# Experts' token tables from one-hot products on TensorE in place of scattered writes, key and query products on two engines, gate logits in column strips

## The chip, the cores and the metric

The kernel runs on one core of one Trainium2 chip. The metric is the device time of one execution in microseconds (us), less is better. The core's engines each run a queue of their own: TensorE (PE; its weight loads are PEld), VectorE (DVE), ScalarE (ACT), GpSimd (POOL) and SyncE (SP), which issues most DMAs. The profile gives one execution; "q" behind an engine (SPq) is its issuing side.

## The reference

Three layers follow each other on 3072 tokens (4 sequences of 768) with 384 features (8 heads of 48):

```python
# attention: a state of 48x48 for each of 32 heads, decayed by alpha
state = alpha[:, :, t, :, None] * state + einsum('bhd,bhe->bhde', k[:, :, t], v[:, :, t])
y[:, :, t] = einsum('bhd,bhde->bhe', q[:, :, t], state)
# mixture of 8 experts: 384 -> 1024 -> 384, two experts for each token
noisy = x @ w_gate + log1p(exp(x @ w_noise)) * noise
top2, weights = two largest of noisy, softmax of the two
for e in range(8):
    out[mask] += weights * (relu(x[mask] @ w1[e]) @ w2[e])
# last layer: 384 -> 2048 -> 384 with a leaky relu
out = max(0.01 * (x @ w_in), x @ w_in) @ w_out
```

## The kernel before

**Order.** A planner (class `Planner`) writes out the order of all engines' queues before anything runs. Each step has an engine (or two to choose from, "vg" for DVE or GpSimd), an expected duration, steps that it waits for, buffers that it takes from rings of a fixed count, and a due time, which is passed back from successors. The planner takes the engine that can start earliest and on it the ready step with the earliest due time. So a changed duration or wait also moves other steps. Queues then run in that order, each instruction waiting for its semaphores. Steps of phase 1 (attention, routing, first gathers) are placed until the last tile has been turned; then phase 2 (experts, last layer) follows, with what is left of phase 1 in between.

**Attention** (phase 1). 24 units of 128 tokens, eight heads each in 112 partitions. For each unit DVE scans the decay backwards (`suf`) and forwards (`wt`, two scans, the second operand in PSUM), and multiplies keys (`kt`, line 918) and queries (`qp`, line 922) by them. TensorE turns the keys (930), makes the scores (943: 48 rows in either half of the array, eight products of 128 columns), updates the state (975, 979) and makes the output `pY` (996 within the unit, 1001 across units). ScalarE copies PSUM to SBUF; GpSimd masks the scores (`am`, 952), decays the state (`sp`, 968) and makes two small products of totals.

**Routing** (phase 1 for six tiles of four units). TensorE turns a tile of x in 12 transposes (1040), ScalarE copies it to `xt` (one buffer), TensorE makes the logits of 16 columns (1050: three products with 512 moving columns), ScalarE copies them, four small transposes bring tokens back to the partitions (1059). A chain of some 30 small steps, most on DVE, picks two experts for each token and, with a triangular product on TensorE (1119, 1120), counts each choice's place in its expert's queue. `si` (1141) is the row of the table that belongs to the choice. GpSimd then writes token numbers with eight indirect DMAs for each tile (1148), 128 numbers each, into the table `idx_d` in DRAM, 48 in all.

**Experts** (phase 2). Each expert has two groups of slots, 384 and 480 rows. SyncE loads the table back (`load_idx`, 505): an early one, of the first four tiles, for the first groups of experts 0 and 1; two later ones for the rest. GpSimd gathers the tokens' rows of x by it (510), TensorE turns them (528), then come the hidden products (668) and the output products (707), in fp32r with every operand split into a high and a low part (three matmuls for one). Rows go to `y_d`; the last layer gathers two rows for each token (730), adds them with the gate's weights and does the same kind of products.

A slot's row in the table is interleaved by blocks: 480 slots are four blocks of 120.

## Time and profile before

| | us |
|---|---|
| median of the 3 timed runs | 1103.73 |
| their lowest and highest | 1098.47, 1114.14 |
| the profiled execution, whole | 1096.46 |
| its span, first to last instruction | 1094.7 |

The span is what the views of the trace show; 1.8 us of the profiled execution lie around it. TensorE's busy time is modelled (pipelined matmuls), so it is read together with its idle time in a stage and with the granted clock, a share of full speed: 1.00 is 2.4 GHz, 0.50 is 1.2 GHz.

### The profile page before, as it was taken

What the parts mean: (1) busy time and instruction counts of PE and PEld (TensorE: products, weight loads), DVE (VectorE), ACT (ScalarE), POOL (GpSimd) and SP (SyncE); (2) the same over time, 40 slices, a digit from 0 to 9 for tenths busy, and PEclk for the clock granted to TensorE, in tenths of its full rate; (3) what the DMA queues carried; (4) which work ended last, traced back from release to release, by engine and by line L of the source; (5) the groups of instructions that cost most, each with busy time, mean ns of one, the idle gap of its engine ahead of it and who ended that gap; (6) DMA issues with size and microseconds to landing.
All of it is one profiled execution on the core that took longest, in us unless ns stands there. A gap on an engine that the chain in (4) does not pass through costs nothing.

```text
span 1094.7 us, 17345 instructions
## 1 busy us (share of the span) xinstructions
PE 1068.6 (98%) x6404; PEld 1017.5 (93%) x6404; DVE 586.8 (54%) x1199; ACT 389.1 (36%) x829; POOL 324.6 (30%) x386
## 2 busy tenths in 40 slices
PE   7999998999999999999999999999999999999997
PEld 6877886899999999999999999999999999999997
DVE  8588974522445554754565334554555555454543
ACT  3665553322344453533453333231222212121211
POOL 3457766531113333444253131320111102010000
PEclk9999896999999999999999999999999999999999
DMA  9868832233345364655566555320101111100000
GB/s 245 239 180 194 176 82 86 39 92 107 121 124 184 125 208 148 209 168 154 172 206 226 198 190 181 115 66 7 59 12 55 29 37 30 37 23 22 1 23 25
DMA packets 76965, 125.76 MB, mean 115 GB/s; under 512 B 10407, under 2 KB 57383, under 8 KB 76871
## 3 DMA queue, kind: packets, MB, share of 16 engines
q1 hardware_dynamic: 68679, 104.47, 31.9%
q0 software_dynamic: 8192, 20.09, 6.5%
q8 instruction: 52, 0.85, 0.3%
q14 instruction: 42, 0.34, 0.1%
HBM read 91.84 MB, written 32.69 MB: 114 GB/s over the span
## 4 chain that ended last, share of the span: by engine, by line
PE 93%; POOL 2%; issue 2%; DVE 1%; ACT 1%; DMA 1%; POOLq 0%; ACTq 0%; DVEq 0%
PE py L707 40%; PE ph L668 39%; PE pY L996 3%; PE pA L528 2%; PE pS L943 2%; PE pY L1001 2%; PE pM L975 1%; PE pA L1050 1%; PE pM L979 1%; DMA at<-in_al_l_dram 1%; PE pM L930 1%; PE pA L1040 1%; POOL am L952 1%; POOL idx_d L1148 1%; DVE kt L918 0%
## 5 line engine op out<-in xcount | busy, mean ns | idle before, releaser
L692 DVE SCALAR_TENSOR_TENSOR hl<-ph,hh 128x384 fp32r<-128x384 f32 (+1 forms) x128 | 77.6, 606 | 202.7 <-ACT hh L685 186.6
L678 ACT ACTIVATE hc<-ph 128x384 f32<-128x384 f32 x128 | 62.9, 492 | 294.9 <-PE ph L668 289.6
L681 DVE SCALAR_TENSOR_TENSOR hc<-hc 128x384 f32<-128x384 f32 x128 | 71.5, 558 | 174.6 <-ACT hc L678 173.0
L685 ACT ACTIVATE hh<-ph 128x384 fp32r<-128x384 f32 (+1 forms) x128 | 68.0, 531 | 261.3 <-PE ph L668 247.8
L707 PE MATMUL py<-w2hA,hh 128*128 128x384 f32 (+1 forms) x416 | 142.1, 342 | 0.0
L707 PE MATMUL py<-w2hB,hh 128*128 128x384 f32 (+1 forms) x416 | 141.7, 341 | 0.0
L707 PE MATMUL py<-w2hA,hl 128*128 128x384 f32 (+1 forms) x416 | 140.5, 338 | 0.0
L707 PE MATMUL py<-w2lA,hh 128*128 128x384 f32 (+1 forms) x416 | 140.2, 337 | 0.0
L707 PE MATMUL py<-w2lB,hh 128*128 128x384 f32 (+1 forms) x416 | 140.0, 337 | 0.0
L707 PE MATMUL py<-w2hB,hl 128*128 128x384 f32 (+1 forms) x416 | 140.0, 337 | 0.0
L668 PE MATMUL ph<-xh,w1hA 128*128 128x384 f32 (+1 forms) x384 | 136.0, 354 | 0.9 <-issue 0.9
L668 PE MATMUL ph<-xl,w1hA 128*128 128x384 f32 (+1 forms) x384 | 134.2, 350 | 0.2 <-issue 0.2
L668 PE MATMUL ph<-xh,w1hB 128*128 128x384 f32 (+1 forms) x384 | 133.9, 349 | 0.0
L668 PE MATMUL ph<-xh,w1lA 128*128 128x384 f32 (+1 forms) x384 | 133.9, 349 | 0.0
L668 PE MATMUL ph<-xl,w1hB 128*128 128x384 f32 (+1 forms) x384 | 133.6, 348 | 0.0
L668 PE MATMUL ph<-xh,w1lB 128*128 128x384 f32 (+1 forms) x384 | 133.5, 348 | 0.0
L730 POOL DMA_INDIRECT xg<-y_d,gidx x48 | 48.7, 1015 | 263.2 <-PE pA L528 212.5
L510 POOL DMA_INDIRECT xg<-x_d,idx x56 | 55.7, 994 | 106.4 <-PE pA L528 87.0
L707 PEld LDWEIGHTS py<-w2hA,hh 128*128 128x128 f32 (+1 forms) x416 | 77.3, 186 | 1.2 <-issue 0.3
L707 PEld LDWEIGHTS py<-w2lA,hh 128*128 128x128 f32 (+1 forms) x416 | 77.3, 186 | 0.9
L707 PEld LDWEIGHTS py<-w2lB,hh 128*128 128x128 f32 (+1 forms) x416 | 77.3, 186 | 1.0
L707 PEld LDWEIGHTS py<-w2hB,hh 128*128 128x128 f32 (+1 forms) x416 | 77.3, 186 | 0.8
(153 smaller groups left out, 1989.0 us busy)
## 6 DMA issues: line engine op xcount, KB each, us to landing
w1s<-in_moe_w_dram SPq DMA_DIRECT2D x32, 384.0 KB
w2s<-in_moe_w_dram SPq DMA_DIRECT2D x32, 384.0 KB
kq<-in_kq_l_dram SPq DMA_DIRECT2D x24, 448.0 KB
w1s<-in_moe_w_in_dram SPq DMA_DIRECT2D x24, 256.0 KB
w2s<-in_moe_w_out_dram SPq DMA_DIRECT2D x16, 384.0 KB
y_d<-ys SPq DMA_DIRECT2D x32, 180.0 KB
at<-in_al_l_dram SPq DMA_DIRECT2D x24, 226.2 KB
nv<-in_v_l_dram SPq DMA_DIRECT2D x24, 192.0 KB
```

The lines of the kernel that those rows point to most:

```text
L510: nc.gpsimd.indirect_dma_start(out=xg[:n, :], out_offset=None, in_=x_d[0:rows, :], in_offset=bass.IndirectOffsetOnAxis(ap=idx_sb[i][:n, j, ...
L528: nc.tensor.transpose(p[:, d, :n], src[:n, d * 128:(d + 1) * 128], identf[:n, :n])
L668: nc.tensor.matmul(ps[:, :n], a[:, d, fo:fo + 128], x[:, d, :n], start=i == 0, stop=i == len(seq) - 1)
L678: nc.scalar.activation(hc[:, :n], ps[:, :n], AF.Copy)
L681: nc.vector.scalar_tensor_tensor(hc[:, :n], hc[:, :n], 0.01, hc[:, :n], op0=OP.mult, op1=OP.max)
L685: nc.scalar.activation(hh[:, :n], ps[:, :n], AF.Relu)
L692: nc.vector.scalar_tensor_tensor(hl[:, :n], ps[:, :n], 0.0, hh[:, :n].bitcast(FT), op0=OP.max, op1=OP.subtract)
L707: nc.tensor.matmul(py[:n, :], h[:, o:o + n], w[:, f % 2, :], start=(f == 0 and i == 0), stop=(f == nf - 1 and i == 2))
L730: nc.gpsimd.indirect_dma_start(out=yg, out_offset=None, in_=y_d[0:rows, :], in_offset=bass.IndirectOffsetOnAxis(ap=gidx[:, c, kk:kk + 1], ...
L943: nc.tensor.matmul(d["pa", i][:, p], d["kt"][r, p], d["qp"][r, p], start=True, stop=True)
L996: nc.tensor.matmul(d["py"][:, p, i * D:(i + 1) * D], d["am"][:, i, p, :], d["v"][:, h * D:(h + 1) * D], start=h == 0, stop=first, skip_gro ...
L1001: nc.tensor.matmul(d["py"][:, p, :], d["qp"][:, p], d["sp"][:, p].rearrange("p s d -> p (s d)"), start=False, stop=True, skip_group_check= ...
```

## The change

- `idx_d`, its zeroing, the scatters and the three index loads are gone. For each tile three integer operations on DVE split the slot number into a row (0 to 127) and a column (block and expert, 56 in all). DVE compares a row of counts with them: one-hot rows (128 wide) and one-hot columns (56 wide) in bf16, for four token columns and two choices. The one-hot columns are multiplied by the token's position in its column of 128 and by the number of that column (DVE or GpSimd). Eight bf16 matmuls sum row x column products over the tile's tokens (`table`), 112 columns; DVE adds the sum to `places`, and one DVE step, `indices`, makes token numbers of it. That step stands where an index load stood: one early, after four tiles, one late.
- The one-hot rows and columns use the one `xt` buffer, and a tile's turning takes that buffer before its first transpose.
- Key and query products may run on DVE or GpSimd, as the planner finds.
- The logits of a tile are made in four strips of 32 columns of the array, one for each unit, 12 products of 128 columns; the gate's weights are padded to 32 columns. One copy of 128x128 and one transpose bring them back.
- 480 slots are three blocks of 128 and one of 96, not interleaved.
- Expected durations for the state's update, logits and copies are changed.

```diff
-    idx_d = dram.tile([1 + E * CAP, 1], I32, name="idx_d")
...
+    NBLK = -(-CAP // 128)
+    tok = consts.tile([128, NCH, 2], FT)
+    count = consts.tile([128, 128], I32)
+    places = consts.tile([128, 2, NBLK * E], FT)
+    idx_sb = [consts.tile([128, NBLK, E], U32, name=f"idx{i}") for i in range(2)]
...
-    GB = [blocks_of(g) for g in GR]
+    GB = [[(o, min(128, g - o)) for o in range(0, g, 128)] for g in GR]
...
-    def load_idx(i, g):
-        src = slots_of(idx_d, g).rearrange("p j e o -> p (j e o)")
-        nc.sync.dma_start(idx_sb[i][:GB[g][0][1]].rearrange("p j e -> p (j e)"), src.bitcast(U32))
+    def indices(i):
+        nc.vector.scalar_tensor_tensor(idx_sb[i].rearrange("p j e -> p (j e)"), places[:, 1], 128.0, places[:, 0],
+                                       op0=OP.mult, op1=OP.add)
...
-        late_in = [add("s", 0.07, lambda g=g: load_idx(g, g), list(scat), lat=2.3) for g in (1, 0)]
+        late_in = add("v", 0.25, lambda: indices(1), list(placed))
...
-            kk = add("v", 0.86, keys, [b1], use=[(LK, R["kq"]), (b0, R["suf"])], takes=[R["kt"]])
-            qq = add("v", 0.9, queries, [f1], use=[(LK, R["kq"]), (f0, R["wt"])], takes=[R["qp"]])
+            kk = add("vg", dict(v=0.86, g=1.35), keys, [b1], use=[(LK, R["kq"]), (b0, R["suf"])], takes=[R["kt"]])
+            qq = add("vg", dict(v=0.9, g=1.35), queries, [f1], use=[(LK, R["kq"]), (f0, R["wt"])], takes=[R["qp"]])
...
-                up = add("p", 0.72, update, use=[(ck, R["kN"]), (LV, R["nv"])], takes=[R["pM"]], due=b + 3.2)
+                up = add("p", 0.9, update, use=[(ck, R["kN"]), (LV, R["nv"])], takes=[R["pM"]], due=b + 3.2)
...
             def logits():
-                k["pl"] = ps2.tile([2 * E, TT], FT, name="pA")
+                k["pl"] = ps2.tile([128, C], FT, name="pA")
                 for d in range(KD):
-                    nc.tensor.matmul(k["pl"], wgn[:, d, :], k["xt"][:, d, :], start=(d == 0), stop=(d == KD - 1))
+                    for c in range(NG):
+                        nc.tensor.matmul(k["pl"][32 * c:32 * c + 32, :], wgn[:, d, :], k["xt"][:, d, c * C:(c + 1) * C],
+                                         start=(d == 0), stop=(d == KD - 1), skip_group_check=True)
...
-                for c in range(NG):
-                    nc.tensor.transpose(k["pb"][:, c, :], k["lt"][:, c * C:(c + 1) * C], identf[:2 * E, :2 * E])
+                nc.tensor.transpose(k["pb"].rearrange("p c e -> p (c e)"), k["lt"], identf)
...
-                tx = add("p", 0.46, lambda d=d: turn_x(d), xs[T] + before, use=[(xs[T][0], R["x"])], takes=[R["pA"]],
-                         due=b + 2 + 2 * d)
+                tx = add("p", 0.46, lambda d=d: turn_x(d), xs[T] + ([t0] if d else before), use=[(xs[T][0], R["x"])],
+                         takes=[R["pA"]] + ([] if d else [R["xt"]]), due=b + 2 + 2 * d)
...
-            lg = add("p", 1.35, logits, [consts_in] + cp, use=[(cp[0], R["xt"])], takes=[R["pA"]], due=b + 8)
-            cl = add("a", 0.6, copy_l, [lg], use=[(lg, R["pA"]), (cp[0], R["xt"])])
-            tb = add("p", 0.35, turn_back, [cl], use=[(cp[0], R["xt"])], takes=[R["pA"]], due=b + 10)
+            lg = add("p", 0.8, logits, [consts_in] + cp, use=[(t0, R["xt"])], takes=[R["pA"]], due=b + 8)
+            cl = add("a", 0.28, copy_l, [lg], use=[(lg, R["pA"]), (t0, R["xt"])])
+            tb = add("p", 0.2, turn_back, [cl], use=[(t0, R["xt"])], takes=[R["pA"]], due=b + 10)
...
-            def scatter(kk, c):
-                ins = nc.gpsimd.indirect_dma_start(
-                    out=idx_d[:, :], out_offset=bass.IndirectOffsetOnAxis(ap=keep["si"][:, kk, c:c + 1], axis=0),
-                    in_=tok[:, c0 + c:c0 + c + 1], in_offset=None, bounds_check=E * CAP, oob_is_err=False)
...
+            def split_slot():
+
+                keep["row"], keep["col"] = (rt.tile([128, 2, n], U32, name=nm) for nm in ("row", "col"))
+                nc.vector.tensor_scalar(keep["row"], keep["si"], 3, 127, op0=OP.logical_shift_right, op1=OP.bitwise_and)
+                nc.vector.tensor_scalar(keep["col"], keep["si"], 10, 3, op0=OP.logical_shift_right,
+                                        op1=OP.logical_shift_left)
+                nc.vector.scalar_tensor_tensor(keep["col"], keep["si"], 7, keep["col"], op0=OP.bitwise_and,
+                                               op1=OP.bitwise_or)
+
+            def one_hot(what):
+                if what == "row":
+                    buf = early.tile([128, KD, TT], FT, name="xt", bufs=1).rearrange("p d c -> p (d c)").bitcast(BF)
...
+                src = keep[what].bitcast(I32)
+                for k in range(2):
+                    nc.vector.tensor_tensor(out[:, k], count[:, None, 0:m].to_broadcast([128, n, m]),
+                                      src[:, k, :, None].to_broadcast([128, n, m]), op=OP.is_equal)
+
+            def numbers(en):
+                eng = nc.vector if en == "v" else nc.gpsimd
+                for k in range(2):
+                    for w in range(2):
+                        eng.tensor_mul(keep["vals"][:, k, :, w, :], keep["cols"][:, k],
+                                       tok[:, c0:c0 + n, w:w + 1].to_broadcast([128, n, NBLK * E]))
+
+            def table():
+                keep["pt"] = ps2.tile([128, 2 * NBLK * E], FT, name="pA")
+                for i in range(2 * n):
+                    k, c = divmod(i, n)
+                    nc.tensor.matmul(keep["pt"], keep["rows"][:, k, c], keep["vals"][:, k, c].rearrange("p w f -> p (w f)"),
+                                     start=i == 0, stop=i == 2 * n - 1)
+
+            def collect():
+                pl = places.rearrange("p w f -> p (w f)")
+                nc.vector.tensor_add(pl, keep["pt"], pl)
...
-            sc = [add("g", 1.29, lambda kk=kk, c=c: scatter(kk, c), [sl] + late, lat=2.2,
-                      due=1e9 if late else at_unit(4 * gr[-1] + 5) + RDUE + 25 + 1.3 * (2 * c + kk)) for c in range(n) for kk in range(2)]
-            scat.extend(sc)
+            kw = {} if late else dict(due=at_unit(4 * gr[-1] + 5) + RDUE + 25)
+            ss = add("v", 0.6, split_slot, [sl], **kw)
+            h0 = add("v", 1.15, lambda: one_hot("row"), [ss], takes=[R["xt"]], **kw)
+            h1 = add("v", 0.6, lambda: one_hot("col"), [ss], use=[(h0, R["xt"])], **kw)
+            nb = add("vg", dict(v=1.2, g=2.0), numbers, [h1], use=[(h0, R["xt"])], **kw)
+            tb = add("p", 0.6, table, [nb], use=[(h0, R["xt"])], takes=[R["pA"]], **kw)
+            co = add("v", 0.25, collect, placed[-1:] + late, use=[(tb, R["pA"])], **kw)
+            placed.append(co)
...
-                early_in = add("s", 0.07, lambda: load_idx(2, 0), list(scat), lat=2.3)
+                early_in = add("v", 0.25, lambda: indices(0), list(placed))
```

## Rows read from the trace of the kernel before

**Rows 1.** The page: busy time of each engine, share of span, instructions.

```profile
PE 1068.6 (98%) x6404; PEld 1017.5 (93%) x6404; DVE 586.8 (54%) x1199; ACT 389.1 (36%) x829; POOL 324.6 (30%) x386
```

**Rows 2.** Stages: length, busy (instructions) of five engines, TensorE clock, DMA, GB/s.

```profile
24.68:163.72 139.04, 133.88 (x1140) 111.02 (x1139) 110.38 (x254) 81.13 (x192) 87.85 (x128) 0.98 0.71 177
111.60:119.50 7.90, 7.90 (x48) 7.01 (x47) 7.52 (x17) 4.69 (x11) 6.57 (x11) 0.57 0.62 120
163.72:182.71 18.99, 16.55 (x105) 15.31 (x105) 9.20 (x33) 4.97 (x11) 10.49 (x13) 0.66 0.08 25
...
182.71:200.36 17.65, 14.17 (x60) 9.32 (x59) 10.03 (x21) 10.81 (x21) 13.47 (x13) 0.78 0.63 165
...
300.00:1085.00 785.00, 785.00 (x4447) 769.19 (x4446) 401.03 (x786) 253.01 (x528) 177.62 (x175) 1.00 0.33 105
```

**Rows 3.** The chain of waits, 66 to 103 us: start, length, what.

```profile
75.92 1.00 POOL idx_d L1148
...
90.23 5.68 DMA at<-in_al_l_dram
```

**Rows 4.** TensorE's timeline, 163 to 200 us: start, length, what, idle before.

```profile
170.31 1.01 PE L930 MATMUL pM<-identf,kt 112*128 112x112 f32 x4 [1.64 <-DVE kt L918]
...
176.68 0.23 PE L1119 MATMUL pA<-ot,tri 128*128 128x32 bf16 x1
176.75 0.19 PE L1120 MATMUL pA<-acc,ones_b 128*128 128x32 bf16 x1
...
190.81 0.42 PE L1059 MATMUL pA<-identf,xt 16*128 16x16 f32 x4 [0.26 <-ACT xt L1054]
...
193.74 0.61 PE L668 MATMUL ph<-xh,w1hA 128*128 128x384 f32 x1 [0.18 <-issue]
```

**Rows 5.** GpSimd's timeline, 170 to 182 us.

```profile
171.45 0.97 POOL L1148 DMA_INDIRECT idx_d<-tok,si  x1 [0.30 <-issue]
...
180.71 0.99 POOL L510 DMA_INDIRECT xg<-x_d,idx  x1 [3.79 <-DMA idx<-idx_d]
```

**Rows 6.** SyncE's waits before 230 us: total, times, longest.

```profile
SPq L505 <- DMA idx_d<-tok,si: 28.4, 1, 28.4
```

**Rows 7.** The chain of waits, 44 to 48 us.

```profile
44.01 1.09 PE pS L943 x16
45.10 2.68 PE pA L1050 x6
```

**Rows 8.** Groups by line, 0 to 170 us: busy, mean ns, idle before.

```profile
L1148 POOL DMA_INDIRECT idx_d<-tok,si x31 | 33.2, 1073 | 9.0 <-issue 5.9 <-DVE si L1141 1.5 <-DVE pC L896 1.0
...
L952 POOL TENSOR_SCALAR_AFFINE_SELECT am<-ar 128x512 f32<-128x512 f32 x46 | 31.4, 691 | 26.9 <-ACT ar L947 26.7
...
L968 POOL TENSOR_TENSOR sp<-S,pend 112x384 f32<-112x384 f32 x20 | 17.1, 857 | 16.0 <-ACT S L984 12.6 <-DMA nv<-in_v_l_dram 3.3
...
L918 DVE TENSOR_TENSOR kt<-kq,suf 112x512 f32<-112x512 f32 x24 | 18.4, 768 | 0.0
...
L922 DVE TENSOR_TENSOR qp<-kq,wt 112x512 f32<-112x512 f32 x23 | 22.0, 956 | 0.1
...
L246 DVE TENSOR_TENSOR g_oh<-g_ca,g_cm 128x32 f32<-128x32 f32 x10 | 4.7, 467 | 0.2
```

**Rows 9.** Timeline of all engines, 95.8 to 99 us.

```profile
95.89 0.82 POOL L968 TENSOR_TENSOR sp<-S,pend 112x384 f32<-112x384 f32 x1
95.92 3.11 DVE L922 TENSOR_TENSOR qp<-kq,wt 112x512 f32<-112x512 f32 x1
...
96.68 1.80 POOL L456 TENSOR_TENSOR w2lA<-w2s,w2hA 128x768 fp32r<-128x768 f32 x1
```

**Rows 10.** The tile wt, 60 to 170 us: duration in ns, least, median, most.

```profile
L897 DVE TENSOR_TENSOR_SCAN wt<-at,pC x28: 686/687/689, 61.1 to 154.4; 112x256 f32<-112x256 f32 x28
```

**Rows 11.** DVE's timeline: slots of the fourth and the fifth tile.

```profile
154.08 0.14 DVE L1141 SCALAR_TENSOR_TENSOR si<-pk,g_cm 128x8 uint32<-128x8 f32 x1
...
178.19 0.17 DVE L1141 SCALAR_TENSOR_TENSOR si<-pk,g_cm 128x8 uint32<-128x8 f32 x1 [0.18 <-DVE pk L1137]
```

More of the change, by code (lines that the diff above doesn't have):

```diff
@@ L395, in tile_kernel @@
     desc = consts.tile([128, E], FT)
-    wgn = consts.tile([128, KD, 2 * E], FT)
+    wgn = consts.tile([128, KD, 32], FT)
     noise_sb = consts.tile([128, NCH, E], FT)
@@ L589, in rows_in @@
                 else:
-                    deps, rows = [late_in[1 - g]] + stored, N
-                GX["a", e, g, j] = add("g", 1.29, lambda j=j, rows=rows: gather1(e, g, j, rows, 2 if rows < N else g), deps, takes=[R["xg"]],
+                    deps, rows = [late_in] + stored, N
+                GX["a", e, g, j] = add("g", 1.29, lambda j=j, rows=rows: gather1(e, g, j, rows, 0 if rows < N else 1), deps, takes=[R["xg"]],
                                        lat=2.0)
@@ L1070, in build_turn @@
                 core.append(tx)
-                cp.append(add("a", 0.61, lambda d=d: copy_x(d), use=[(tx, R["pA"])] + ([(cp[0], R["xt"])] if d else []),
-                              takes=[] if d else [R["xt"]]))
-            lg = add("p", 1.35, logits, [consts_in] + cp, use=[(cp[0], R["xt"])], takes=[R["pA"]], due=b + 8)
-            cl = add("a", 0.6, copy_l, [lg], use=[(lg, R["pA"]), (cp[0], R["xt"])])
-            tb = add("p", 0.35, turn_back, [cl], use=[(cp[0], R["xt"])], takes=[R["pA"]], due=b + 10)
+                t0 = t0 if d else tx
@@ L1140, in slots @@
                 keep["si"] = rt.tile([128, 2, n], U32, name="si")
-                nc.vector.scalar_tensor_tensor(keep["si"], keep["pk"], 0.0, keep["cm"], op0=OP.add, op1=OP.add)
+                nc.vector.scalar_tensor_tensor(keep["si"], keep["pk"], -1.0, keep["cm"], op0=OP.add, op1=OP.add)
             link("v", small + 0.05, chosen)
@@ L1145, in build_route @@
             sl = link("v", 0.19, slots, more=done_of.get(gi - 2, []))
-            def scatter(kk, c):
-                ins = nc.gpsimd.indirect_dma_start(
-                    out=idx_d[:, :], out_offset=bass.IndirectOffsetOnAxis(ap=keep["si"][:, kk, c:c + 1], axis=0),
-                    in_=tok[:, c0 + c:c0 + c + 1], in_offset=None, bounds_check=E * CAP, oob_is_err=False)
-                for other in scattered:
-                    tc.declare_no_dep(ins.ins, other.ins, reason="every choice has a slot of its own")
-                scattered.append(ins)
+            def split_slot():
[5 more added lines that the diff above has]
+                                               op1=OP.bitwise_or)
@@ new lines, in one_hot @@
+            def one_hot(what):
+                if what == "row":
+                    buf = early.tile([128, KD, TT], FT, name="xt", bufs=1).rearrange("p d c -> p (d c)").bitcast(BF)
+                    w = 2 * n * 128
+                    keep["rows"] = buf[:, 0:w].rearrange("p (k c r) -> p k c r", k=2, c=n)
+                    keep["vals"] = buf[:, w:w + 4 * n * NBLK * E].rearrange("p (k c w f) -> p k c w f", k=2, c=n, w=2)
+                    w += 4 * n * NBLK * E
+                    keep["cols"] = buf[:, w:w + 2 * n * NBLK * E].rearrange("p (k c f) -> p k c f", k=2, c=n)
+                out = keep[what + "s"]
+                m = out.shape[3]
+                src = keep[what].bitcast(I32)
+                for k in range(2):
+                    nc.vector.tensor_tensor(out[:, k], count[:, None, 0:m].to_broadcast([128, n, m]),
+                                      src[:, k, :, None].to_broadcast([128, n, m]), op=OP.is_equal)
@@ L1165, in build_route @@
                 link(eng, 0.2 if fn.__name__ != "r" else 0.4, fn)
-            done_of[gi] = [chain[-1]] + sc
+            done_of[gi] = [chain[-1], ss, h0, h1]
             done_of["chain", gi] = chain
@@ L1187, in tile_kernel @@
                 rc = add("g", 6.0, route_consts, due=at_unit(2))
-                zr = add("s", 0.07, zero_idx, [rc], lat=2.5, due=at_unit(4))
+                zr = add("s", 0.07, zero_row, [rc], lat=2.5, due=at_unit(4))
             T, c = divmod(u, NG)
@@ L1295, in general @@
                 for d in range(KD):
-                    nc.tensor.matmul(pl[:, c, :], xt[:, d, c * 128:(c + 1) * 128], wgn[:, d, :], start=(d == 0),
+                    nc.tensor.matmul(pl[:, c, :], xt[:, d, c * 128:(c + 1) * 128], wgn[:, d, 0:2 * E], start=(d == 0),
                                      stop=(d == KD - 1))
@@ L1397, in _laid_out @@
     wgn = _np.concatenate([inputs["moe_w_gate"], inputs["moe_w_noise"]], 1)
+    wgn = _np.pad(wgn, ((0, 0), (0, 32 - wgn.shape[1])))
     n, e = inputs["moe_noise"].shape
@@ L1402, in _laid_out @@
         "v_l": _np.ascontiguousarray(inputs["v"].transpose(0, 2, 1, 3)).reshape(b * s, h * d),
[L1403 removed]
+        "wgn_l": _np.ascontiguousarray(wgn.reshape(-1, 128, 32).transpose(1, 0, 2)),
         "noise_l": _np.ascontiguousarray(inputs["moe_noise"].reshape(n // 128, 128, e).transpose(1, 0, 2)),
```

47 lines of the change are left out of this document (22 added, 25 removed).

## The prediction

> **What bounds the kernel now.** I read the page's busy times first: TensorE is busy for 98% of the span and no other engine for more than 54% [rows 1]. So the question is what the change does to TensorE's work, waits and clock. The busy times by stage come next [rows 2]. From 300 to 1085 us TensorE is busy 785.00 of 785.00 us at a granted clock of 1.00: the experts and the last layer. The change alters nothing that these matmuls read, in number or shape of stream, so about 895 us are out of its reach. What can move lies before 200 us, in three stretches:
>
> - A, from the scores of the third unit to those of the 23rd: 139.04 us for 20 units, 6.95 each. TensorE is idle 139.04 - 133.88 = 5.2 us. In 111.6 to 119.5 its granted clock is 0.57 (it was at 2.4 GHz before, and here at 1.2), which costs 7.9 x 0.43 = 3.4 us. Lost: 8.6 us.
> - B, from there to the turning of the last tile: 18.99 us, idle 2.4, clock 0.66 over 16.55 busy us, 5.6 more. Lost: 8.0 us.
> - C, to the third hidden product: 17.65 us, idle 3.5, clock 0.78 over 14.17, 3.1 more. Lost: 6.6 us.
>
> The chain of waits tells who ends the waits in A: between 66 and 103 us it runs over GpSimd, through the scatters of token numbers, and over a late load [rows 3]. TensorE's own timeline shows B and C: it waits 1.64 us for the keys of the last unit, after which the clock is low in B, and the first hidden product starts at 193.74, 11 us after C begins [rows 4]. Why so late: the last scatter of the early table ends at 172.4, the index load behind it lands 3.8 us after GpSimd stands idle, and the first gather starts at 180.71 [rows 5]. SyncE waited 28.4 us for that scatter [rows 6].
>
> **The change part by part.**
>
> *Logits in strips.* Today three products with 512 moving columns are six matmuls in 2.68 us; four transposes bring them back. The change makes 12 products of 128 columns into four column strips, and one transpose. No row shows column strips. The nearest is the scores: 8 products of 128 columns that alternate between two halves of the array's rows take 1.09 us [rows 7], 0.136 each; 12 of them are 1.64 us. The ends: no overlap, 2.68 us or slightly more; all four strips at once, a quarter, 0.67. I take 1.64, as the operands alternate in the same way. The Trainium skill ("TensorEngine Tiling (Array Packing)", section "Theoretical Speedup") gives up to 4x for 32 columns; by it the logits would be 0.67 us and the sum 5 us better; no row here shows a column strip. The four transposes take 0.42 us [rows 4]; one is about 0.11. So a tile loses 1.04 + 0.3 us of TensorE.
>
> *Tables on TensorE.* Each tile adds 8 bf16 matmuls of 112 columns. The bf16 matmuls of the positions, whose weights are 128x128 too, take 0.19 to 0.23 us alone and follow each other after 0.07 [rows 4]; 8 x 0.09 = 0.7 us, ends 0.5 and 1.8. Net per tile: -1.04 - 0.3 + 0.7 = -0.64; five tiles lie before the experts: **-3 us** (ends -9 and +5).
>
> *Their DVE work.* Per tile: three small integer operations (si is 0.14 to 0.17 [rows 11]), two comparisons of 128x512, two of 128x224, four multiplications of 128x224 and one addition. Keys, 112x512 with two operands, take 0.77 us on average, queries 0.96 [rows 8]. So 0.5 + 2 x 0.7 + 2 x 0.35 + 0.3 = 2.9 us, and 1.4 more if DVE does the multiplications: 0.7 to 1.1 us per unit. DVE is busy 110.38 of 139.04 us in A [rows 2], 5.5 per unit. If both products went to GpSimd, 1.7 us per unit would leave it. DVE falls to some 4.9, under TensorE's 6.8: **0 us**, hidden behind TensorE. If the products all stay, it is 6.6 and the cover is nearly gone.
>
> *GpSimd.* 31 scatters leave in the first 170 us: 33.2 us and 5.9 of issue. A product of 112x512 there costs, by sp (112x384 in 0.857), 1.14 us, and by w2lA (128x768 in 1.80 [rows 9]) 1.20; I take 1.17. 24 units bring 28 us (one product each) to 56. So GpSimd ends between 11 us less and 17 us more loaded; the gain is that no product has to stand in a row of scatters. Behind a product in its queue stand the masks (am), which the second half of each unit waits for, and the states' decay (sp), 0.69 and 0.86 us [rows 8]. That is why I give A **half of its loss back, -4 us** (ends -8.6 and +6, 0.3 us a unit, the price of one more mask's wait in every other unit).
>
> *DVE against GpSimd.* The row that speaks against moving products: qp on DVE, 0.96 us on average, took 3.11 us from 95.92, while sp and w2lA ran on GpSimd to 98.48 [rows 9]. The scans, whose second operand lies in PSUM, never stretch: 686 to 689 ns in 28 [rows 10]. So DVE instructions with two SBUF operands stand still while GpSimd computes. The Trainium skill ("SBUF — State Buffer", "Who interferes with whom") says the same of two SBUF inputs against a GpSimd instruction that reads SBUF; by that rule, which the trace bears out, the new comparisons and the gate's steps would wait behind each product on GpSimd; its price is the third and fourth case below.
>
> *The end of the attention.* The keys that TensorE waits for in B [rows 4] can now run on GpSimd, but the products there also stretch others. I give B **half back, -4 us** (ends -8 and 0).
>
> *Early table.* No scatter, no index load, no wait of SyncE; weights and x_d stores queued behind that wait go early. The slots of the fourth tile are known at 154.08 [rows 11]; splitting, comparisons, numbers, table and addition add 4 to 6 us with their hops, so the gathers can start near 160 instead of 180.71, and end before the attention does. C loses its cause: **two thirds back, -4.5 us** (ends -6.6 and 0).
>
> *The shared buffer.* The one-hot rows take the xt buffer, of which there is one. A tile's turning and the table of the tile before exclude each other; the last tile's turning may stand behind the fourth's or fifth's table, up to 5 us. The fifth tile's slots come at 178.19 [rows 11]; with 4 to 6 us its table would be done at 183, and the last turning begins at 182.71: they can meet, and who comes first is open. **+1 us** (0 to +5). On TensorE everything is queued behind that turning.
>
> *No cost taken:* new constants (a few short instructions of GpSimd ahead of the first tile), blocks of 128, 128, 128 and 96 rows instead of four of 120 (as many matmuls, 384 columns each), two later tables (the experts' first two groups need only the early one).
>
> **Sum:** -3 - 4 - 4 - 4.5 + 1 = -14.5 us. The profiled execution took 1096.46 us (span 1094.7); that gives 1082. The median of the runs shown is 1103.73, 7 us above it, and their lowest 2 us above: I add 3 us and say **1085**, own range 1076 to 1095.
>
> **Rivals.**
>
> *All of it comes back.* The clock stays at 2.4 GHz through B and C, strips overlap in fours. For it: with no wait of over 1 us at 168 the half clock of B might not come. Against: DVE and GpSimd still hold each other up. -8.6 - 8 - 6.6 - 5 = -28: about 1071 with the same 3 us. Chance 0.22.
>
> *It does not do what it says.* Strips run one after the other, so TensorE gains nothing per tile and pays 0.7 - 0.3 us for the table (+2), products wait as long as they did behind scatters, and only C gives something: -4 + 2 = -2, 1095 to 1105. For it: each strip's weights are loaded anew, and GpSimd's load is not smaller. Chance 0.22.
>
> *Slower: DVE becomes the bound.* With both products on GpSimd it computes two masks, the decay and two products, 1.4 + 0.9 + 2.3 = 4.6 us per unit. Every DVE step with two SBUF operands, some 26 per tile or 6.5 per unit, may then wait. Such waits exist today: g_oh, of 32 elements, averages 0.47 us [rows 8] where si, of 8, takes 0.14 to 0.17 [rows 11]. DVE would need 5.5 - 1.7 + 1.1 = 4.9 us per unit, today's waits included; it passes today's pace of 6.95 when the mean wait grows by 0.3 us, and the whole is slower by 22 us from 0.5 us on: 4.9 + 3.3 = 8.2, 1.2 a unit more, 24 units, +29 less the 4.5 of C: about 1123. Against: scans, half of DVE's time, never wait. Chance 0.07.
>
> **How the numbers follow.** Forecast 0.49, the rivals 0.22, 0.22 and 0.07. Two per cent, 22 us, is about what a measurement of this kernel can tell from no change. Faster by more: the first rival and a little of the forecast's low end, 0.27. Slower by more: 0.06. The rest, 0.67, is within. The range takes in the first rival's time and the second's: 1068 to 1106; about 0.1 lies on each side.
>
> **What would show it.** Right: logits of 24 matmuls in some 1.6 us; kt or qp on GpSimd at 1.2 us; the first gather before 170 us; the first hidden product near 180; granted clock over 0.8 from 164 to 182; 6.7 us per unit in A. Wrong: TensorE waiting for kt, qp or am several times per tile with two-operand steps on DVE stretched; the last turning waiting for a table; logits still at 2.7 us; or anything after 300 us that moves.

## The result and the profile after

The changed kernel takes 1114.91 us (median of 20 runs, 1105.51 to 1126.82), the kernel before 1104.49 in the same sessions: ratio 1.0087, 95% interval 1.0058 to 1.0117. I had forecast 1085 and a range to 1106. The 20 runs fall in two groups, nine at 1105.5 to 1107.8 us and eight at 1114.2 to 1116.1, with three longer ones: the median lies in the upper group, the profiled execution in the lower. The profiled execution takes 1107.1 us, span 1105.3, mean granted clock 0.976 (before 1094.7 and 0.986).

The page's busy row, beside [rows 1]: TensorE has 138 more instructions and is as busy.

```profile
PE 1070.0 (97%) x6542; PEld 1028.8 (93%) x6542; DVE 602.3 (54%) x1232; ACT 387.7 (35%) x829; POOL 316.7 (29%) x381
```

Busy time by stage, columns as in [rows 2]: the attention from the scores of the sixth to those of the 23rd unit, four stretches in it and behind it, and the experts.

```profile
44.41:184.82 140.41, 119.63 (x1084) 106.71 (x1083) 113.75 (x266) 70.75 (x170) 80.68 (x114) 0.85 0.49 148
78.07:93.00 14.93, 14.78 (x80) 13.60 (x80) 14.38 (x38) 3.85 (x9) 7.75 (x12) 0.51 0.28 81
111.20:124.00 12.80, 5.83 (x38) 5.17 (x39) 11.53 (x16) 3.22 (x10) 9.30 (x6) 0.60 0.45 119
141.90:148.00 6.10, 6.05 (x39) 5.00 (x40) 4.00 (x11) 2.28 (x6) 3.90 (x8) 0.55 0.27 78
183.40:196.00 12.60, 12.53 (x74) 11.41 (x74) 5.40 (x27) 2.70 (x6) 6.35 (x7) 0.59 0.16 48
300.00:1085.00 785.00, 785.00 (x4443) 766.69 (x4442) 402.27 (x782) 256.15 (x533) 177.41 (x175) 1.00 0.34 107
```

From 300 us on nothing has moved; from the first hidden product to the last instruction it takes 899.1 us (901.0 before, 899 to 903 in every run below). The loss is in the attention: 17 units take 140.41 us, 8.3 each, where 20 took 139.04 before. TensorE is idle for 20.8 us of it and runs at a mean clock of 0.85. TensorE's own timeline shows the new parts and the waits:

```profile
69.98 0.86 PE L1053 MATMUL pA<-xt,wgn 128*32 128x128 f32 x24
70.78 1.16 PE L944 MATMUL pS<-qp,kt 48*128 48x128 f32 x16
71.87 0.33 PE L1062 MATMUL pA<-identf,xt 128*128 128x128 f32 x1
72.03 1.03 PE L1002 MATMUL pY<-sp,qp 112*128 112x96 f32 x8
72.90 0.55 PE L931 MATMUL pM<-identf,kt 112*128 112x112 f32 x4
78.07 1.01 PE L931 MATMUL pM<-identf,kt 112*128 112x112 f32 x4 [4.62 <-DVE kt L919]
...
81.33 0.93 PE L1185 MATMUL pA<-xt 128*128 128x112 bf16 x8
82.05 1.26 PE L997 MATMUL pY<-nv,am 128*128 128x48 f32 x5
...
205.31 1.09 PE L1041 MATMUL pA<-identf,x 128*128 128x128 f32 x8 [0.59 <-DVE xl L538]
206.16 0.42 PE L669 MATMUL ph<-xh,w1hA 128*128 128x384 f32 x1
```

The 24 logits matmuls take 0.80 us from their start to the next instruction's, the table 0.72, and the first hidden product follows at once on the last turning, where before it came 11 us behind the start of that turning [rows 4]. These parts did what they should. But ahead of the keys of one unit TensorE waits 4.62 us for VectorE, and then works at 1.2 GHz for 15 us (the row 78.07:93.00, clock 0.51). It happens four times: waits of 4.62, 7.04, 2.30 and 2.52 us. (A fifth stretch at 1.2 GHz, 100 to 104 us with a clock of 0.50, follows a wait of only 0.63 us.) The longest, on three engines:

```profile
110.66 1.81 POOL L460 TENSOR_TENSOR w1lA<-w1s,w1hA 128x768 fp32r<-128x768 f32 x1 [1.62 <-ACT w1hA L456]
110.81 0.33 PE L1062 MATMUL pA<-identf,xt 128*128 128x128 f32 x1 [0.69 <-ACT xt L1058]
111.17 5.27 DVE L1171 TENSOR_TENSOR xt<-count,row 128x512 bf16<-128x512 int32 x2 [0.69 <-PE pA L1062]
112.43 1.71 POOL L923 TENSOR_TENSOR qp<-kq,wt 112x512 f32<-112x512 f32 x1
114.10 1.79 POOL L460 TENSOR_TENSOR w2lA<-w2s,w2hA 128x768 fp32r<-128x768 f32 x1
115.86 1.70 POOL L919 TENSOR_TENSOR kt<-kq,suf 112x512 f32<-112x512 f32 x1
116.37 1.75 DVE L919 TENSOR_TENSOR kt<-kq,suf 112x512 f32<-112x512 f32 x1
...
118.17 1.01 PE L931 MATMUL pM<-identf,kt 112*128 112x112 f32 x4 [7.04 <-DVE kt L919]
```

The two comparisons of the one-hot rows (0.68 us each where nothing disturbs them) take 5.27 us while GpSimd runs splits and a query product, and the keys that TensorE waits for stand behind them. The groups by line, 0 to 170 us, give the products' price on either engine, beside [rows 8]:

```profile
L919 POOL TENSOR_TENSOR kt<-kq,suf 112x512 f32<-112x512 f32 x11 | 14.4, 1306 | 1.8 <-DMA kq<-in_kq_l_dram 1.8
L923 POOL TENSOR_TENSOR qp<-kq,wt 112x512 f32<-112x512 f32 x9 | 14.0, 1556 | 0.0
L923 DVE TENSOR_TENSOR qp<-kq,wt 112x512 f32<-112x512 f32 x12 | 9.8, 819 | 5.5 <-PE pY L1002 5.4
L919 DVE TENSOR_TENSOR kt<-kq,suf 112x512 f32<-112x512 f32 x10 | 9.2, 916 | 0.0
L1171 DVE TENSOR_TENSOR xt<-count,row 128x512 bf16<-128x512 int32 x6 | 7.8, 1347 | 0.7 <-PE pA L1062 0.7
```

Three theories for the loss. *Queue*: the one-hot steps stand ahead of the next unit's products on VectorE. *GpSimd*: the products there stretch VectorE's steps and come late. *Clock*: the waits are mostly slack that the shorter TensorE work made, and what costs is the half clock behind them.

### The profile page after: what moved, and what is told of

Its sections match the earlier page's. It is cut to its first block, busy times and chain, and to the rows that moved or that the text cites. A ratio compares the mean times of both kernels' runs of the same rounds, so it can differ in the third digit from the quotient of the medians.

```text
span 1105.3 us, 17577 instructions
## 1 busy us (share of the span) xinstructions
PE 1070.0 (97%) x6542; PEld 1028.8 (93%) x6542; DVE 602.3 (54%) x1232; ACT 387.7 (35%) x829; POOL 316.7 (29%) x381
## 4 chain that ended last, share of the span: by engine, by line
PE 92%; DVE 6%; issue 1%; ACT 1%; POOL 0%; DMA 0%; SPq 0%; POOLq 0%; ACTq 0%; DVEq 0%
PE py L708 40%; PE ph L669 39%; PE pY L997 3%; PE pS L944 2%; PE pA L529 2%; PE pM L976 2%; PE pY L1002 1%; DVE xt L1171 1%; PE pM L980 1%; PE pM L931 1%; DVE suf L889 1%; DVE wt L898 1%; PE pA L1041 1%; DVE kt L919 0%; DVE qp L923 0%
## 5 line engine op out<-in xcount | busy, mean ns | idle before, releaser
L696 DVE TENSOR_TENSOR hl<-hc,hh 128x384 fp32r<-128x384 f32 x128 | 71.5, 559 | 12.2 <-DVE hh L688 0.9
```

The source lines that it names most:

```text
L696: nc.vector.tensor_sub(hl[:, :n], HT[si, "hc"][:, :n], hh[:, :n].bitcast(FT))
```

## The experiments

### Cutting the one-hots, moving the products back, strips alone

*hot_separate* and *hot_cut* keep every queue's order and give the one-hots a buffer of their own; the second also leaves out all but one column of each.

```diff
-  buf = early.tile([128, KD, TT], FT, name="xt", bufs=1)...
+  buf = hot                       # cleared at the start
...
+  m = 1                           # hot_cut only
-  nc.vector.tensor_tensor(out[:, k], count...
+  nc.vector.tensor_tensor(out[:, k, :, 0:m], count...
```

> Changed kernel with every queue in the same order, but the one-hots in a buffer of their own instead of the buffer that holds the turned tile. Queue theory (the slot steps stand in VectorE's queue ahead of the next unit's key and query products, so their time lands on TensorE): nothing changes, 1110 to 1117 us, the four waits of TensorE for kt and qp stay. GpSimd theory (products and token numbers on GpSimd stretch VectorE's two-operand steps): nothing changes either. Buffer theory (the one-hots wait for the shared buffer, or the turning waits for them): the wait ahead of the long one-hot goes, 1100 to 1106 us.

> As the run with the separate buffer, same order of every queue, but each one-hot writes 1 of its 128 (or 56) columns into a buffer cleared at the start, so that nearly all of VectorE's one-hot time goes; the token tables come out wrong. Queue theory: some 2.1 us undisturbed and up to 6 us stretched go per tile ahead of kt and qp, TensorE's waits of 4.6, 7.0 and 2.3 us shrink to under half and the half clock behind them with it: 1095 to 1104 us. GpSimd theory: the products still stretch whatever VectorE does meanwhile; at most 4 us go, 1108 to 1115 us. Order theory (the planner's other order of TensorE's queue and the start are what costs): no change, 1110 to 1117 us.

*products_vector_same_order*: the planner still believes in two engines, the instruction goes to VectorE.

```diff
- (nc.vector if en == "v" else nc.gpsimd).tensor_mul(d["kt"], ...
+ nc.vector.tensor_mul(d["kt"], ...          # queries alike
```

> Changed kernel with the same order of steps, but the 23 key and query products that it has on GpSimd run on VectorE, at the same places of the order. GpSimd theory: VectorE's two-operand steps are no longer stretched, the products take 0.87 instead of 1.3 to 1.5 us, the 7 us wait near 111 us goes: 1096 to 1106 us. Queue theory: VectorE, 113.75 us busy of the 140.41 that hold the attention, gets 20 us more: 1112 to 1125 us.

*strips_only*: the kernel before with the diff's hunks of the logits, nothing else.

> Kernel before with the logits in four column strips and one transpose back, all else as before: products on VectorE, scatters on GpSimd. Both theories: logits fall from 2.68 to about 0.8 us and the turning back from 1.7 to 0.3, six tiles, 10 to 18 us less work of TensorE: 1086 to 1098 us where TensorE is the bound of the attention; if GpSimd's scatters or VectorE hold the attention instead, no change (1101 to 1106).

Measured, against the kernel before: hot_separate 1114.36 us, 1.0087 (1.0040 to 1.0134): the shared buffer costs nothing that shows. hot_cut 1099.50, 0.9942 (0.9902 to 0.9981): the one-hots' time on VectorE is worth 15 us. (Its tables are wrong, but behind the first hidden product it takes 900.5 us as the others do.) products_vector_same_order 1100.82, 0.9942 (0.9900 to 0.9983): the products on GpSimd are worth 14 us, although VectorE has to make 23 more of them. The queue theory alone had said slower. Both gains are differences of medians; between the profiled executions they are 7.5 and 9.6 us (1107.1 to 1099.62 and to 1097.53). And the waits shrank less than I had expected: the one of 7.04 us is still 6.14 in hot_cut and 4.91 in products_vector_same_order. The rows of products_vector_same_order, in the same window as above:

```profile
L923 DVE TENSOR_TENSOR qp<-kq,wt 112x512 f32<-112x512 f32 x22 | 17.2, 780 | 4.8 <-PE pY L1002 4.8
L919 DVE TENSOR_TENSOR kt<-kq,suf 112x512 f32<-112x512 f32 x22 | 15.5, 703 | 0.0
L1171 DVE TENSOR_TENSOR xt<-count,row 128x512 bf16<-128x512 int32 x6 | 4.7, 830 | 0.0
```

strips_only: 1107.25, 0.9984 (0.9946 to 1.0023), just above the range of its no-change branch and with no gain from matmuls that are 1.9 us shorter in each of six tiles. Four stretches of its windows, and two lines of its TensorE ahead of the third:

```profile
88.00:104.00 16.00, 16.00 (x87) 14.59 (x86) 6.77 (x18) 6.85 (x14) 6.78 (x13) 0.50 0.78 183
128.00:132.00 4.00, 2.19 (x17) 1.82 (x17) 3.93 (x8) 0.98 (x2) 2.97 (x5) 1.00 0.84 103
136.00:144.00 8.00, 8.00 (x66) 6.26 (x68) 5.68 (x13) 3.89 (x9) 4.21 (x5) 0.58 0.80 186
152.00:180.00 28.00, 27.33 (x143) 25.20 (x140) 18.27 (x45) 10.04 (x24) 16.11 (x24) 0.50 0.34 66
```

```profile
132.19 0.18 PE L1121 MATMUL pA<-acc,ones_b 128*128 128x32 bf16 x1 [2.00 <-DVE acc L1111]
...
134.93 0.98 PE L930 MATMUL pM<-identf,kt 112*128 112x112 f32 x4 [0.95 <-DVE kt L918]
```

TensorE, with less to do, waits 2.00 and 0.95 us for VectorE, and falls to 1.2 GHz for the third stretch; the fourth follows waits of 0.63 and 0.23 us at 148 and lasts 28 us of full work at that clock. What the strips saved is given back there (the table near the end: 35.4 us lacking, 15.3 in the kernel before).

### Filling the waits; each other part alone; a better order

*fill_waits* changes only TensorE's queue:

```diff
+ for p in range({10: 28, 13: 42, 22: 14}.get(u, 0)):      # ahead of the keys' turning
+     nc.tensor.transpose(d["pk"][:, p % HP, :], identf[:PP, :], identf[:PP, :PP])
...
+ for p in range({17: 12}.get(u, 0)):                      # ahead of the scores
+     nc.tensor.transpose(d["pa", 0][:, p % HP], identf, identf)
```

> Changed kernel, same queues, and in TensorE's queue transposes of the identity whose results are overwritten, 28, 42 and 14 of them ahead of the turning of the keys of units 10, 13 and 22 and 12 ahead of unit 17's scores: they fill the four waits (4.62, 7.04, 2.52 and 2.30 us) and compute nothing that is used. Clock theory (the waits themselves are mostly slack; what costs is that TensorE runs at 1.2 GHz for 6 to 15 us after each): granted clock near 1.00 through the attention, 1095 to 1102 us. Wait theory (the waits themselves are the loss): no change, 1106 to 1116 us, or slower by up to 10 us where the waits are shorter than the filling. Both need the clock to answer to transposes whose result nobody reads; if it does not, no change either, and the clock row shows it.

*tables_only*: the changed kernel with the logits of the kernel before and products on VectorE. *products_only*: the kernel before with the two lines below as in the change. *own_late_vector*: the changed kernel with

```diff
- kk = add("vg", dict(v=0.86, g=1.35), keys, ...           # queries alike
+ kk = add("v", 0.86, lambda: keys("v"), ...
- takes=[R["xt"]]                                          # one-hots, numbers, table
+ takes=[R["hot"]]
- due=at_unit(4 * gr[-1] + 5) + RDUE + 25
+ due=at_unit(4 * min(gr[-1] + 2, EARLY_TILES) + 5) + RDUE + 25
```

> Kernel before with the token tables alone: logits 2.68 us wide and products on VectorE as before, orders planned anew. Slot theory (the one-hot steps on VectorE hold up the products whatever else is done): attention 8 to 15 us longer, 1103 to 1112 us. Clock and GpSimd theory (VectorE's steps stay short without products on GpSimd, TensorE keeps its longer logits work and so its clock; the gathers' late start, two thirds of 6.6 us, goes): 1090 to 1100 us.

> Kernel before with the key and query products planned on two engines, nothing else changed. GpSimd theory: products of 1.3 to 1.5 us on GpSimd in place of 0.87, in a queue that also holds 32 scatters, masks and decays, and VectorE's two-operand steps stretched: 1108 to 1120 us. Queue theory (VectorE relieved of some 20 us): 1095 to 1104 us.

> Changed kernel with products on VectorE only, the one-hots in a buffer of their own, and the one-hot steps due two tiles later, so that the next units' products go first. All theories but the clock: VectorE no longer ahead of TensorE with slot steps, TensorE's shorter logits show: 1080 to 1092 us. Clock theory: TensorE with 11 us less work waits in small pieces, and granted half clock gives 5 to 10 us of it back, as in the run with strips alone: 1090 to 1102 us.

Measured: fill_waits 1104.74 us, 0.9997 (0.9963 to 1.0032), 10 us under the changed kernel by the medians, with every useful instruction the same (the two profiled executions differ by 1.3 us only); its attention, in the same stretch as above, has a clock of 0.90 for 0.85. It fell short of the 1095 to 1102 expected: the filling was shorter than the waits (2.17, 4.28 and 1.11 us of the first, second and fourth are left), and half clock still follows the first three. The third wait, 2.29 us, was not filled at all: it stands ahead of the scores of unit 16 (the code counts from 0), and the 12 transposes ahead of unit 17 run from 151.30 us on, where nothing waited.

```profile
44.41:184.82 140.41, 125.62 (x1173) 112.20 (x1173) 114.25 (x261) 69.82 (x169) 79.18 (x113) 0.90 0.50 148
```

tables_only 1091.33, 0.9884 (0.9829 to 0.9940). products_only 1123.70, 1.0170 (1.0111 to 1.0229). own_late_vector 1085.95, 0.9824 (0.9777 to 0.9871). So the tables gain 13 us, the strips nothing, and the products on two engines lose 19 of the kernel before. How, in products_only, on three engines:

```profile
91.54 2.81 DVE L209 TENSOR_TENSOR g_um<-g_um,g_ru 128x32 f32<-128x32 f32 x1 [0.61 <-ACT g_ru L205]
...
92.24 1.28 POOL L922 TENSOR_TENSOR qp<-kq,wt 112x512 f32<-112x512 f32 x1
...
96.01 0.67 DVE L918 TENSOR_TENSOR kt<-kq,suf 112x512 f32<-112x512 f32 x1
...
96.73 1.01 PE L930 MATMUL pM<-identf,kt 112*128 112x112 f32 x4 [2.13 <-DVE kt L918]
```

A step of 32 elements takes 2.81 us beside GpSimd's work, the keys in the queue behind it come late, TensorE waits 2.13 us, and its granted clock is 0.50 from 96 to 120 us.

### What GpSimd's work does: three ghosts

Products on VectorE in the changed kernel's order, and at the 23 places of GpSimd's queue work for nobody, about as long as a product (1.3 to 1.4 us):

```diff
+ if en == "g":
+     nc.gpsimd.tensor_mul(ghost, d["kq"][:, 0], d["sv"])                  # two inputs
+     nc.gpsimd.affine_select(out=ghost, in_=d["kq"][:, 0], ...); (... in_=d["sv"], ...)   # one input each
+     for _ in range(3): nc.gpsimd.memset(ghost...[:, 0:448], 0.0)         # writes only
  nc.vector.tensor_mul(d["kt"], ...
```

> As the run with the products on VectorE in the same order (1100.8 us), but at the 23 places of GpSimd's queue the same product is formed a second time into a scratch tile that nobody reads. Port theory (two-operand steps of GpSimd and of VectorE hold each other up, so that VectorE's steps stretch): the time of the changed kernel comes back, 1108 to 1118 us, VectorE's steps longer. Lateness theory (what costs is only that a key or query product comes 0.4 to 0.7 us later from GpSimd, or behind its queue): nobody waits for the copies, 1099 to 1104 us.

> The control of the run with ghost products: at the same 23 places GpSimd makes two selects of one input each (0.69 us a piece by the masks' rows, so 1.4 us, as long as a product) into the scratch tile. Port theory: VectorE is not stretched, 1098 to 1105 us, below the run with ghost products by 8 us or more. If GpSimd's queue being fuller is what costs (masks and decays late), both ghost runs are equally slow, 1105 to 1118 us. Lateness theory: both 1099 to 1104 us.

> Third ghost: products on VectorE in the changed kernel's order (1100.8 us), and at the 23 places of GpSimd's queue three clears of the scratch tile (448 columns each, about 0.47 us by the clears of the start, together as long as a product): GpSimd is as full, but reads nothing. The Trainium skill (SBUF — State Buffer, Who interferes with whom) has VectorE's steps of two SBUF inputs contend with GpSimd instructions that read SBUF, not with those that only write it. By that, VectorE's other work up to the slots of the fourth tile stays near 114 us (122.4 and 119.0 with the ghosts that read two and one input), and the time near 1101 us, 1097 to 1106. Full queue theory (masks and decays come late behind whatever GpSimd does): 1112 to 1125 us, as with the other ghosts.

For these runs VectorE's timeline is summed up from its start to the same instruction, the splitting of the fourth tile's slots (durations of its rows in us; where rows overlap, both count):

```
run                          products on VectorE  other steps  time of the run (median)
products_vector_same_order   30.9 (42)            114.0        1100.82
after                        19.0 (22)            122.0        1114.91
ghost_two_inputs             39.5 (42)            122.4        1125.41  1.0233 (1.0181 to 1.0284)
ghost_one_input              36.4 (42)            119.0        1123.03  1.0175 (1.0116 to 1.0235)
ghost_writes_only            31.8 (42)            115.5        1113.59  1.0071 (1.0030 to 1.0113)
```

Both ghosts that read are slower than any of their theories had (1118 us at most). Moving 20 products off VectorE took 11.9 us from it, and 8.0 came back as longer other steps. Ghosts that read stretch VectorE, with one input too, so the select was no control for the port; the ghost that only writes hardly does (1.5 us). That agrees with the Trainium skill (SBUF — State Buffer, Who interferes with whom): VectorE's steps with two SBUF inputs contend with GpSimd instructions that read SBUF, not with those that only write. But its time did not stay: 1113.59, where that theory had 1097 to 1106. One of TensorE's waits in it, the same place in hot_separate, which has no ghosts, and then the stretch of its attention:

```profile
102.23 3.62 PE L1004 MATMUL pY<-nv,am 128*128 128x48 f32 x16 [0.63 <-POOL ghost L922]
```

```profile
101.81 3.62 PE L999 MATMUL pY<-nv,am 128*128 128x48 f32 x16 [0.63 <-POOL pend L908]
```

```profile
44.41:184.82 140.41, 125.92 (x1017) 112.89 (x1016) 102.85 (x253) 67.04 (x159) 71.13 (x136) 0.76 0.49 147
```

So a fuller GpSimd queue costs even where it hardly stretches VectorE: 12.8 us over products_vector_same_order, in intervals that do not meet. How, no run shows. In the profiled executions the whole difference is the clock's (34.5 us lacking for 17.5, in the table further down). TensorE's waits do not explain it: those of over 0.9 us, from 44 us to the first hidden product, sum to 13.0 us with these ghosts and to 13.1 without, and the wait of 0.63 us stands in hot_separate too. TensorE is at half clock from 76 to 112 us, where products_vector_same_order was back at 1.00 near 92; but hot_separate, without ghosts, also stays low there, and the changed kernel's profiled execution was back at 1.00 near 92 and low again only from 99. So that stretch cannot be put down to the ghosts.

### Order, start, and the best version

*products_vector* is the changed kernel with the products planned on VectorE (the first two lines of the diff above); *gpsimd_in_vector_order* has its order and 24 products on GpSimd; *two_engines_from_unit_4* plans two engines for units 4 to 23 alone; *own_late_filled* adds filling transposes to own_late_vector.

```diff
+ lambda: keys("v" if u % 2 else "g")        # gpsimd_in_vector_order, queries the other way round
...
+ "vg" if u >= 4 else "v"                    # two_engines_from_unit_4
...
+ range({13: 7, 16: 8, 19: 14, 22: 6}.get(u, 0))    # own_late_filled, and 11 ahead of unit 15's outputs
```

> Changed kernel with the products planned on VectorE alone, so that the planner makes its order for that; strips, tables and the shared buffer as in the change. Against tables alone (1091.3 us) it has the strips added, against the run with own buffer and later one-hots (1086.0 us) the shared buffer and the earlier due times. If the parts simply add, 1088 to 1092 us. Buffer theory: the shared buffer costs 3 to 10 us here, 1089 to 1097 us. Clock theory: strips make holes in TensorE's work and half clock eats their gain, 1089 to 1096 us with a clock row below that of tables alone.

> The run with products planned on VectorE (1088.3 us), every queue in that order, but 24 of the 48 products (keys of even units, queries of odd ones) executed on GpSimd. Against the same swap in the changed kernel's own order, where GpSimd's 23 products cost 14 us. Stretch theory (GpSimd's work lengthens VectorE's other steps, 8.0 us of them up to the slots of the fourth tile, and the products come late): 10 to 18 us here too, 1098 to 1106 us. Order theory (the products cost only in the order that the planner makes for two engines): 1086 to 1092 us.

> Changed kernel with the products of units 0 to 3 planned on VectorE and those of the other 20 on two engines. Start theory: the half clock of the start ends near 24 us as in the kernel before, and not near 35 us, unit 5 is scored at 38 or 39 and not at 44 us, and 5 us come back: 1105 to 1111 us. If the start's 5 us are made up or lost again by the later waits: 1111 to 1117 us.

> The fastest version so far (own buffer, later one-hots, products on VectorE, 1086.0 us) with transposes whose results are overwritten in the five waits of its TensorE (7, 8, 14 and 6 ahead of the keys of units 13, 16, 19 and 22, 11 ahead of unit 15's outputs; waits of 1.13, 1.29, 2.17, 1.09 and 1.66 us). Clock theory: the stretches at 1.2 GHz from 116 to 120 and from 138 to 155 us go, 1076 to 1082 us. Wait theory: no change, 1083 to 1088 us.

Measured: products_vector 1088.34 us, 0.9863 (0.9816 to 0.9910). gpsimd_in_vector_order 1100.44, 0.9951 (0.9917 to 0.9985): 12 us for the engine in this order, 14 in the other; the order itself is worth 12.5 and 14.5. Here 44 products on VectorE take 35.2 us and the other steps 112.8 up to the fourth slots; with 22 of them on GpSimd 18.7 and 123.9. two_engines_from_unit_4 1106.44, 1.0041 (1.0003 to 1.0080). Scores in TensorE's timeline, changed kernel first:

```profile
27.55 2.08 PE L944 MATMUL pS<-qp,kt 48*128 48x128 f32 x16
```

```profile
24.74 1.16 PE L944 MATMUL pS<-qp,kt 48*128 48x128 f32 x16
...
38.38 1.16 PE L944 MATMUL pS<-qp,kt 48*128 48x128 f32 x16
```

Scores of 2.08 us are scores at half clock: it ends 10 us earlier, the sixth unit is scored at 38.38 instead of 44.41, and the median falls by 8.5 us, though the intervals overlap. In the profiled execution the 6 us are lost again: its first hidden product starts at 208.30, the changed kernel's at 206.16.

own_late_filled 1084.80, 0.9810 (0.9761 to 0.9858): granted clocks of 0.995 to 0.998 for 0.987 to 0.992, and no gain in the median that can be told from own_late_vector's; it lies in the wait theory's range. The profile shows why that is no verdict on the clock theory. First own_late_vector's scores of the sixth, the 13th and the 23rd unit, then own_late_filled's:

```profile
38.16 1.16 PE L945 MATMUL pS<-qp,kt 48*128 48x128 f32 x16
...
85.18 1.16 PE L945 MATMUL pS<-qp,kt 48*128 48x128 f32 x16
...
168.66 1.16 PE L945 MATMUL pS<-qp,kt 48*128 48x128 f32 x16
```

```profile
51.56 2.08 PE L949 MATMUL pS<-qp,kt 48*128 48x128 f32 x16
...
103.22 1.16 PE L949 MATMUL pS<-qp,kt 48*128 48x128 f32 x16
...
179.09 1.16 PE L949 MATMUL pS<-qp,kt 48*128 48x128 f32 x16
```

In this execution (1096.42 us; two of the six take that long, the others 1077.78 to 1084.97) the start's half clock lasts to about 60 us instead of 24, ahead of the first filling and with every queue as in own_late_vector. That costs it 13 us by the sixth unit. Behind it, where the filling stands, ten units take 75.87 us for 83.48: 7.6 us less with the same useful work. Both versions are 18 us or more under the kernel before and some 29 or more under the changed one.

## Why the prediction was wrong

**The step that failed** is *GpSimd*: "the gain is that no product has to stand in a row of scatters. ... That is why I give A half of its loss back, -4 us (ends -8.6 and +6 ...)". By itself that part costs +19 us (products_only), and +27 in this kernel (1114.9 for 1088.3), far outside the ends. Without that term the sum is -10.5, which is 1089 with my 3 us; the change without that part took 1088.34. That agreement is partly luck: the -4 us of *The end of the attention* rested on the moved products as well, without them the sum gives 1093, and alone the strips gained nothing and the tables 13 us.

*Their DVE work, 0 us, hidden behind TensorE*, failed with it. It counted busy time per unit, and by busy time VectorE is still not the bound (113.75 of 140.41 us). But the steps come in a burst per tile, ahead of the next unit's products; stretched by GpSimd they outlast TensorE's cover, and hot_cut shows 15 us for them by the medians. Where the products stay on VectorE, the cover holds: tables_only is faster.

*DVE against GpSimd* named the mechanism and I left it to the rival of 7 in 100. It was right in kind: 8.0 us of stretch up to the fourth slots. But that is some 0.4 us a unit, where its sum wanted 2 us (6.95 less 4.9) before VectorE would bind: it too counted per unit and not per burst. The runs add what it lacked: a GpSimd queue filled with writes costs 12.8 us with hardly any stretch, in a way that stays open.

*The clock* I reckoned only where it was already low. Half speed for t us loses t/2, so (1 - granted clock) x span is the full-speed time that a run lacks:

```
profiled run                 span     clock  lacking  rest
before                       1094.7   0.986   15.3    1079.4
after                        1105.3   0.976   26.5    1078.8
products_vector_same_order   1095.8   0.984   17.5    1078.3
ghost_writes_only            1112.6   0.969   34.5    1078.1
ghost_two_inputs             1122.6   0.961   43.8    1078.8
strips_only                  1107.5   0.968   35.4    1072.1
tables_only                  1086.6   0.993    7.6    1079.0
own_late_vector              1084.2   0.987   14.1    1070.1
```

In these eight the rest differs by 9 us and the lacking part by 36; over all seventeen profiles the rest lies between 1066 and 1090, the upper end being products_only, own_late_filled (its long start does not show in the clock column) and fill_waits (1088.5, with its added transposes). The changed kernel's whole loss of 10.6 us is there (11.2). Its 20 runs say the same: most have spans of 1104 to 1106 us at clocks of 0.976 to 0.979 or 1112 to 1114 at 0.969 and 0.970; 25 and 34 us lacking, nine apart like the spans. Three do not fit, with spans of 1118.3, 1118.6 and 1125.0 at 0.979.

This is an accounting; that the clock is a cause and not company shows in own_late_filled's 7.6 us, in fill_waits' median, and in two executions with the same order of every queue. The changed kernel's and hot_separate's stay within 0.3 us of each other up to 92.5 us, through the same wait of 4.62 us. Then the first one's clock rises and the second's stays at 0.50 until about 113:

```profile
93.42 1.16 PE L944 MATMUL pS<-qp,kt 48*128 48x128 f32 x16
```

```profile
94.20 2.08 PE L946 MATMUL pS<-qp,kt 48*128 48x128 f32 x16
```

By the turning back of the next logits (110.81, 117.23) hot_separate is 6.4 us late, and the next wait for keys takes up only 1.5 of it (5.55 us for 7.04). Where waits are longer, more of it is slack: in the two profiled executions fill_waits lacks 11 us less than the changed kernel, for a span shorter by 1.3.

*Logits in strips* was mis-sized, 1.64 us for the measured 0.80, nearer to the fourfold of the Trainium skill ("TensorEngine Tiling (Array Packing)", "Theoretical Speedup") than to my row of the scores; with the one transpose a tile saves 1.4 us net, not 0.64. It gave nothing where it made TensorE wait, and 3 us between tables_only and products_vector, which their intervals don't tell from zero.

*Early table* was right in its end, not in its way: the first hidden product follows the last turning, but the gathers start at 184.46, not near 160: the fourth tile's slots come at 170.67 instead of 154.08, and from there it takes 13.8 us instead of 4 to 6. *The shared buffer* was right: small. *The end of the attention* was lost to the fourth wait (2.52 us, clock 0.59 from 183.4 to 196).

**Open**: why TensorE stays at half clock until about 35 us in the nine profiles with an order for two engines, when in the changed kernel it works without a gap from 7.67 us, and until 24 us in seven others. The order alone does not set it, as own_late_filled's 60 us show. Also open are where the rest of that order's 12 to 14 us lies, why the clock rises in one execution near 92 us and not in another, and how a queue of writes on GpSimd costs 12.8 us.

## What to carry to other kernels

Before moving work to an engine that has time, look at what its neighbour does meanwhile: 11.9 us moved off VectorE brought 8.0 back as stretch, and the moved products took 1.3 to 1.6 us instead of 0.7 to 0.9. Sum an engine's cover per burst and queue place, not per average unit. And where TensorE is nearly the bound, work taken from it may open waits that cost its clock: take the work out of the engine that it would then wait for first.

## What was not expected of the hardware

TensorE stays at 1.2 GHz for far longer than the waits ahead of it last: 28 us of full work in strips_only, behind waits of 0.63 and 0.23 us, and 36 in ghost_writes_only from 76 to 112, behind one of 4.47 and with one of 0.63 in between. Behind the same wait of 4.62 us it rose near 92 us in one execution and near 113 in another. Transposes whose result nobody reads keep the clock up too (0.90 for 0.85 in fill_waits). In the first 24 to 35 us, once 60, the profile's clock column shows 1.00 while scores take 2.08 instead of 1.16 us, so the start's clock is read from durations. The changed kernel's row for 28 to 32 us:

```profile
28.00:32.00 4.00, 4.00 (x28) 3.78 (x27) 2.09 (x4) 1.59 (x4) 1.08 (x4) 1.00 1.02 280
```

The DMA load (1.02) does not explain the slow scores: in the kernel before it is 1.09 in the same 4 us, and scores take 1.16. And in the tiles' logits 24 fp32 matmuls in four strips of 32 columns do in 0.80 us what 6 of 512 columns did in 2.68.
